# A fused attention and gated-MLP block: a fourth gate/up tile taken out of the attention's filler, GpSimd's sums moved, masks merged, SyncE's DMA issues in written order

## The chip, the cores and the metric

The kernel runs on one core of a Trainium2 chip. Its engines work side by side, each on a queue of its own: TensorE (PE; PEld is its weight load), VectorE (DVE), ScalarE (ACT), GpSimd (POOL), and SyncE (SP), which here issues most of the DMAs. The metric is the device time of one execution in microseconds (us), as a median of several executions; lower is better.

## What is computed

The reference is one transformer block on 2048 tokens of width 640, in float32:

```
xn  = layernorm(x)                                  # no weights
out = x + attention(xn) + mlp(xn)

attention: 32 heads of width 20; a query sees itself and the 255 keys before it
           softmax(q k^T / sqrt(20) under that band mask) v, then @ wo
mlp:       (gelu(xn @ w_gate) * (xn @ w_up)) @ w_down   # inner width 1728, tanh gelu
```

## The kernel before

Every float32 product is made of three products of split operands: a high part and a low part, high x high, low x high and high x low (`dense_steps`, L103). A projection of 640 inputs is five matmuls of 128 rows for each of the three, 15 in all. The 2048 tokens are four chunks of 512. A name such as xh or wqh is a high part, xl or wql the low one.

**Front.** Layer norm and transposes of the four chunks into xh and xl; query/key tiles 0 and 5 are projected for chunks 0 to 2, and the first values.

**Attention** (`attention`, L803) runs 32 units: 8 groups of four heads by 4 chunks. A unit has 14 slots. Its steps are: maxima of the scores (`max_pair`, L473, matmuls L492 on TensorE, reductions L502 on VectorE), the scores again with the maximum taken off and their exponentials in three banks X, Z and Y (`exp_piece`, L543, matmuls L557, ScalarE L559), masks on GpSimd (`clear`, L565, affine_select L572 on the diagonal and L575 on the band's tail), the products with the values (`av_unit`, L578, L600), copies of the sums by ScalarE, their join on GpSimd (L610) and the store (L614, L615). Between these steps the loop pulls matmuls out of a generator, the **filler** (`filler`, L690). It yields the rest of the query/key tiles (five for queries, five for keys, each by four chunks, L107 with ps_d), the values (ps_v), and some of the 14 gate/up tiles of the MLP (`gate_up_fill`, L646). RATE is how many filler matmuls a unit pulls. Before unit 0 there is a **ramp** of twelve slots (L812) with 2 x RAMP = 8 filler matmuls each and up to two maxima pairs in every other slot, and then GAP more filler matmuls.

The order of TensorE, ScalarE, VectorE and GpSimd in this stage is written out by hand (`manual_schedule`, L858): each engine executes in the order in which the code emits. `defer(n, fn)` emits fn n slots later. SyncE's order is left to the framework's scheduler in this stage; in the two later stages it is in written order as well.

A projected query/key tile is saved in three bf16 parts (`save_qk`, L248): ScalarE copies the high part (L277), VectorE takes it off into r (L273), ScalarE copies the middle part (L255), GpSimd makes the lowest one (L259), SyncE stores all three to DRAM (L268). r has one buffer, the target pt has two, and the PSUM tag dn, in which the filler's projections accumulate, has two (`psd`). The loop's loads of query and key parts for unit u+3 (`load_stack`, L458, DMA L467) are emitted in slots 9 and 12 of unit u; those of units 0 to 2 stand ahead of the ramp. Query/key weights are split by ScalarE (L99) and GpSimd (L100) in one piece of 640 columns for tiles 1 and 6, and later ones in five pieces on GpSimd (L641).

GpSimd also makes **sums** of token chunks (`x_sums`, L727, L738): for each of two pairs p of chunks, eighty tensor_tensor operations of 128x256 in all, forty for each pair. Results go to DRAM as td (store L742). The tile tx, in which they are made, has two buffers.

**Pair loop** (`gate_up_pair`, L939, matmuls L957): the gate/up tiles that weren't in the filler, from number NFA to 12. It reads td, and computes two chunks at a time for a gate and an up tile with seven products for eight, so that a call has 54 matmuls of 128x128 by 128x512 where the direct way takes 60. Two calls make a tile. The last gate/up tile (number 13, half wide) is computed at the start of this stage (`gate_up`). Then comes the **down projection** (L1224), in a similar scheme with quarter sums.

Of the kernel before, what the change touches and what calls it, by code (L numbers as in the profile page):

```python
# [13 lines left out]
OP = mybir.AluOpType  # L14
# [16 lines left out]
NS = 14  # L31
RATE = 30.9
LAST = 8
# [3 lines left out]
LAG = 3, 5, 4, 4, 4, 4, 3, 3, 4, 3, 2, 1, 1, 1  # L37
NFA = 3
HD = D // 2
# [3 lines left out]
WARM = 64  # L43
XS0, XSN = 2, 3
HELD = 10, 11, 12
RAMP = 4.0
GAP = 16
VW = 1408
# [19 lines left out]
def block_kernel(ctx, tc, x, wqk, wv, wgu, wdo, wdl, out):  # L68
# [150 lines left out]
    def defer(n, fn, *a):  # L219
        if now[0] is None:  # L220
            fn(*a)
        else:
            at(now[0] + n, fn, *a)
# [24 lines left out]
    def save_qk(t, c, ps):  # L248
# [9 lines left out]
        def lowest():  # L258
            nc.gpsimd.tensor_tensor(out=pt[:, l, :], in0=r, in1=pt[:, 1, :], op=OP.subtract)  # L259
            defer(1, store)  # L260

# [262 lines left out]
    def pieces(c):  # L524
        b = 4 * c
        X = [(b, 0, 0, 384)] + ([(b - 2, 384, 0, 128)] if c else [])
        Y = [(b + 1, 0, 128, 384), (b + 3, 384, 384, 128)]
        Z = ([(b - 1, 0, 0, 256)] if c else []) + [(b + 2, 256, 256, 256)]
        return X, Z, Y

# [34 lines left out]
    def clear(u, bi, js):  # L565
        c = u % NC
        pt = pts[u, bi]
        for p in pieces(c)[bi]:
            for col, diag in diag_tail(*p, c):
                a, n = pt[:, js, col:col + 128], js.stop - js.start  # L570
                if diag:
                    nc.gpsimd.affine_select(out=a, in_=a, pattern=[[0, n], [1, 128]], compare_op=OP.is_ge,  # L572
                                            fill=0.0, base=0, channel_multiplier=-1)
                else:
                    nc.gpsimd.affine_select(out=a, in_=a, pattern=[[0, n], [-1, 128]], compare_op=OP.is_ge,  # L575
                                            fill=0.0, base=-1, channel_multiplier=1)

    def av_unit(u):  # L578
# [38 lines left out]
        defer(3, join)  # L617
        defer(5, store)

# [26 lines left out]
    def gate_up_fill(f, ws, c):  # L646
# [24 lines left out]
        def c5():  # L671
            if now[0] is not None and st.get("tanh", now[0]) >= now[0]:
                defer(1, late, c5)
                return
            nc.vector.scalar_tensor_tensor(st["t"], st["t"], 1.0, st["g"], op0=OP.add, op1=OP.mult)
            defer(1, lambda: nc.sync.dma_start(hd[f][c], st["t"]))

# [12 lines left out]
    def filler():  # L690
# [6 lines left out]
        for s, (kind, i) in enumerate(sets[:-1]):  # L697
            nxt = []
            after = sets[s + 1]
            for c in range(NC):  # L700
                if kind == "qk":
                    if i == 1 and c < 2:
                        for t in range(8 + 4 * c, 12 + 4 * c):
                            yield from proj_v(v0, t)
                    yield from proj_qk(i, ws[0], c)
                    if i == 2 or i == 3 and c == 0:
                        next(prep)
                    yield from proj_qk(i + 5, ws[1], c)
                    if i == 3 and c == 0:
                        next(prep)  # L710
                else:
                    yield from gate_up_fill(i, ws, c)
# [14 lines left out]
    def x_sums(p, k, half):  # L727
# [12 lines left out]
        def store(i):  # L740
            t = live[i]
            defer(2, lambda: nc.sync.dma_start(td[p][i][:, k, half * w:half * w + w], t))  # L742

# [59 lines left out]
    def attention():  # L803
# [4 lines left out]
        for i, (p, k, half) in enumerate((p, k, half) for p in range(NC // 2) for k in range(2) for half in range(2)):  # L808
            for j, fn in enumerate(x_sums(p, k, half)):
                m = 10 * i + j  # L810
                at(NS * (XS0 + m // XSN) + m % XSN, fn)
        for i in range(12):  # L812
# [44 lines left out]

    with tc.manual_schedule(engines=MANUAL | {mybir.EngineType.Pool}):  # L858
        attention()
# [648 lines left out]
```

## Time and profile before

| | us |
|---|---|
| three runs | 1051.27, 1046.38, 1047.88 |
| median | 1047.88 |
| the profiled execution | 1047.3 |
| its span in the profile | 1045.6 |
| mean granted TensorE clock in it | 0.998 |

The stages of the profiled execution, by the matmuls in the chain of work: the front up to some 62.7 us, the ramp to 93.5, the attention's units to 546.3, number 13 to 560.1, the pair loop to 805.1, the down projection to the end at 1045.6.

How to read the rows: a row of the timeline has a start, a duration, the engine, the line of the kernel, the operation with its output and inputs, shapes and a count; in brackets stands how long the engine was idle before it and what released it. "SPq" is SyncE's queue of DMA issues: the row shows the issue, not the transfer. A row of a group has busy time and mean duration in ns behind the first bar, and idle time before these instructions behind the second, with its releasers. A row of waits has the time in all, how often, and the longest. Durations of merged rows overlap a little at their ends, so that a rate is read from the starts of two rows.

### The profile page before, as it was taken

The numbers are of one execution on the slowest core, as the hardware profiler recorded it, in microseconds if no ns is written. First come the engines' busy times: TensorE is split into PE (matmuls) and PEld (weight loads), VectorE is DVE, ScalarE is ACT, GpSimd is POOL, SyncE is SP. The second block draws the span as 40 slices with busy tenths as digits, with TensorE's granted clock in tenths as the row PEclk, the third lists the DMA queues.
The fourth block names the chain that finished last, engine by engine and source line by source line (L and its number), as shares of the span: only waits on it lengthen the run. The fifth ranks groups of instructions, "written<-read, shape, count | busy, mean of one in ns | idle before, by whom it ended". The sixth has DMA issues, their size and how long they took to land.

```text
span 1045.6 us, 25699 instructions
## 1 busy us (share of the span) xinstructions
PE 1033.1 (99%) x9393; PEld 835.1 (80%) x9393; DVE 743.2 (71%) x2018; ACT 527.8 (50%) x1120; POOL 384.5 (37%) x622
## 2 busy tenths in 40 slices
PE   8999999999999999999999999999999999999998
PEld 7887666666787666666678888888888999999998
DVE  7845666677656576777736788775556888888887
ACT  4434666667666666666675232223234554433432
POOL 5122687979766787767470111101110000000000
PEclk9999999999999999999999999999999999999999
DMA  5642355564633364434125575763217874433333
GB/s 193 190 144 93 102 158 170 160 186 141 190 94 100 111 182 139 131 100 148 61 77 194 176 250 205 255 240 113 80 54 252 271 247 136 137 127 121 115 126 105
DMA packets 105192, 158.76 MB, mean 152 GB/s; under 512 B 15420, under 2 KB 60092, under 8 KB 105064
## 3 DMA queue, kind: packets, MB, share of 16 engines
q1 hardware_dynamic: 102680, 150.95, 44.9%
q10 hardware_dynamic: 2384, 6.16, 1.9%
q8 instruction: 74, 1.21, 0.5%
q14 instruction: 54, 0.44, 0.1%
HBM read 101.78 MB, written 54.92 MB: 150 GB/s over the span
## 4 chain that ended last, share of the span: by engine, by line
PE 94%; DVE 4%; ACT 1%; DMA 1%; issue 1%; SPq 0%; POOL 0%; DVEq 0%; ACTq 0%
PE ps_g L957 23%; PE ps L1224 23%; PE ps_d L107 20%; PE ps_e L557 8%; PE ps_v L107 6%; PE ps_o L600 5%; PE ps_m L492 5%; DVE junk L502 2%; PE ps_g L107 1%; DMA wr<-wqk 1%; PE ps_t L185 1%; PE ps_d L356 0%; DVE r L273 0%; DVE xl L194 0%; ACT P L559 0%
## 5 line engine op out<-in xcount | busy, mean ns | idle before, releaser
L502 DVE CUSTOM_DVE_ANT_0 junk<-ps_m,mask 128x320 bf16<-128x320 f32 (+2 forms) x512 | 242.7, 474 | 129.8 <-PE ps_m L492 71.9
L559 ACT ACTIVATE P<-ps_e 128x512 f32<-128x512 f32 (+2 forms) x384 | 198.7, 572 | 69.3 <-PE ps_e L557 68.8
L1224 PE MATMUL ps<-wb,at 128*128 128x320 f32 x999 | 155.9, 309 | 0.0
L1224 PEld LDWEIGHTS ps<-wb,at 128*128 128x128 f32 x999 | 148.9, 188 | 0.2
L572 POOL TENSOR_SCALAR_AFFINE_SELECT P<-P 128x256 f32<-128x256 f32 (+1 forms) x192 | 94.1, 492 | 73.4 <-ACT P L559 70.7
L557 PE MATMUL ps_e<-qs,ks 124*128 124x128 bf16 (+2 forms) x704 | 118.3, 278 | 0.1
L107 PE MATMUL ps_d<-xl,wqh 128*128 128x512 f32 x310 | 98.4, 421 | 0.0
L107 PE MATMUL ps_d<-xh,wqh 128*128 128x512 f32 x310 | 98.2, 421 | 0.0
L107 PE MATMUL ps_d<-xh,wql 128*128 128x512 f32 x310 | 97.6, 418 | 0.0
L100 POOL TENSOR_TENSOR wql<-wr,wqh 128x640 fp32r<-128x640 f32 x12 | 19.2, 1604 | 195.6 <-PE ps_g L957 151.0
L1224 PE MATMUL ps<-wt,at 128*128 128x320 f32 x552 | 88.9, 309 | 0.0
L557 PEld LDWEIGHTS <-ks 124*128 124x128 bf16 x704 | 49.5, 98 | 49.0 <-issue 34.3
L1224 PEld LDWEIGHTS ps<-wt,at 128*128 128x128 f32 x552 | 82.9, 188 | 0.1
L575 POOL TENSOR_SCALAR_AFFINE_SELECT P<-P 128x512 f32<-128x512 f32 (+1 forms) x144 | 76.4, 538 | 16.3 <-ACT P L559 14.6
L1178 ACT ACTIVATE at<-ss 128x512 fp32r<-128x512 f32 x59 | 37.3, 632 | 83.7 <-DVE ss L1062 83.6
L600 PE MATMUL ps_o<-P,v 64*32 64x320 f32 (+4 forms) x2816 | 74.2, 347 | 0.0
L259 POOL TENSOR_TENSOR pt<-r,pt 128x512 bf16<-128x512 f32 x40 | 46.5, 1164 | 67.2 <-ACT pt L255 61.0
L600 PEld LDWEIGHTS ps_o<-P,v 64*32 64x32 f32 x2816 | 50.9, 106 | 21.5 <-issue 0.9
L492 PE MATMUL ps_m<-ks,qs 60*64 60x320 bf16 (+3 forms) x1472 | 64.9, 260 | 3.1 <-DVE mx L502 1.5
L107 PEld LDWEIGHTS ps_d<-xh,wql 128*128 128x128 f32 x310 | 56.0, 189 | 10.1 <-issue 0.9
L492 PEld LDWEIGHTS <-qs 60*64 60x64 bf16 x1472 | 29.2, 105 | 43.6 <-issue 38.0
L107 PEld LDWEIGHTS ps_d<-xh,wqh 128*128 128x128 f32 x310 | 56.0, 189 | 9.7 <-issue 1.6
(195 smaller groups left out, 1968.4 us busy)
## 6 DMA issues: line engine op xcount, KB each, us to landing
hr<-hd SPq DMA_DIRECT2D x104, 128.0 KB
hd<-he SPq DMA_DIRECT2D x50, 256.0 KB
wr<-wgu SPq DMA_DIRECT2D x27, 320.0 KB
qs<-qd SPq DMA_DIRECT2D x64, 120.0 KB
ks<-kd SPq DMA_DIRECT2D x64, 120.0 KB
xi<-x SPq DMA_DIRECT2D x16, 320.0 KB
qs<-qd SPq DMA_DIRECT2D x64, 80.0 KB
ks<-kd SPq DMA_DIRECT2D x64, 80.0 KB
```

The costliest lines, as they stand in the source:

```text
L107: nc.tensor.matmul(ps, a(k), b(k), start=n == 0, stop=n == 3 * nk - 1)
L259: nc.gpsimd.tensor_tensor(out=pt[:, l, :], in0=r, in1=pt[:, 1, :], op=OP.subtract)
L492: nc.tensor.matmul(ps[64 * h:64 * h + 64, col:col + w], q[rows, j, q0:q0 + 64], ks_, start=True, stop=True, tile_position=(64 * r, 64 * h))
L502: nc.vector.tensor_tensor_reduce(out=junk[:, 0:n], in0=ps[:, 320 - n:320], in1=mask[:, 320 - n:320], scale=1.0, scalar=NEG, op0=OP.add, op ...
L557: nc.tensor.matmul(ps[:, col:col + n], k[0:QROWS, j, kc:kc + 128], q[0:QROWS, j, q0:q0 + n], start=True, stop=True)
L559: nc.scalar.activation(pt[:, j, lo:hi], ps[:, lo:hi], AF.Exp, scale=SCALE)
L572: nc.gpsimd.affine_select(out=a, in_=a, pattern=[[0, n], [1, 128]], compare_op=OP.is_ge, fill=0.0, base=0, channel_multiplier=-1)
L575: nc.gpsimd.affine_select(out=a, in_=a, pattern=[[0, n], [-1, 128]], compare_op=OP.is_ge, fill=0.0, base=-1, channel_multiplier=1)
L600: nc.tensor.matmul(os[r][32 * j:32 * j + 32, qa:qb], v[rows, w0_:w0_ + 32], pt[rows, j, col + qa - q0:col + qb - q0], start=r not in begun ...
L957: nc.tensor.matmul(ps, i, j, start=first and n == 0, stop=n == len(work) - 1, skip_group_check=True)
L1178: nc.scalar.activation(hi[:, 3:7], s, AF.Copy)
L1224: nc.tensor.matmul(ps[bank][:, 0:HD], *work[bank][j], start=bank not in begun, stop=final[p, bank] == n and j == len(work[bank]) - 1, skip ...
```

## The change

- NFA goes from 3 to 2: the filler computes gate/up tiles 0 and 1 (beside the query/key tiles and the values), and tile 2 goes to the pair loop, which now starts there. (With number 13, whose weights the filler splits, there were four sets of gate/up weights in it, now three.)
- RATE goes from 30.9 to 26.95 and GAP from 16 to 24.
- In the filler, the values' projections of token tiles 8 to 15 came ahead of query/key tiles 1 and 6 of chunks 0 and 1; now they come behind those of chunks 1 and 2.
- The forty sums of the first pair move from the units into the ramp, three in each slot from slot -13 on; those of the second start in unit 12. Before, all eighty stood three to a unit from unit 2 on.
- `clear` merges the selects of a bank with the same mask into one with a further axis; the two pieces of bank Y change places so that two diagonal blocks lie side by side.
- SyncE's issues in the attention are in written order too, and the stores of query/key parts, of the attention's sums, of the MLP's inner values and of the second pair's token sums are emitted one or two slots later; those of the first pair one slot earlier.

```diff
-RATE = 30.9
+RATE = 26.95
-NFA = 3
+NFA = 2
-XS0, XSN = 2, 3
+XS0, XSN = 12, 3
-GAP = 16
+GAP = 24
...
         def lowest():
             nc.gpsimd.tensor_tensor(out=pt[:, l, :], in0=r, in1=pt[:, 1, :], op=OP.subtract)
-            defer(1, store)
+            defer(3 if now[0] and now[0] > 0 else 1, store)
...
-        Y = [(b + 1, 0, 128, 384), (b + 3, 384, 384, 128)]
+        Y = [(b + 1, 128, 128, 384), (b + 3, 0, 384, 128)]
...
     def clear(u, bi, js):
         c = u % NC
         pt = pts[u, bi]
-        for p in pieces(c)[bi]:
-            for col, diag in diag_tail(*p, c):
-                a, n = pt[:, js, col:col + 128], js.stop - js.start
-                if diag:
-                    nc.gpsimd.affine_select(out=a, in_=a, pattern=[[0, n], [1, 128]], compare_op=OP.is_ge,
-                                            fill=0.0, base=0, channel_multiplier=-1)
-                else:
-                    nc.gpsimd.affine_select(out=a, in_=a, pattern=[[0, n], [-1, 128]], compare_op=OP.is_ge,
-                                            fill=0.0, base=-1, channel_multiplier=1)
+        cuts = sorted(x for p in pieces(c)[bi] for x in diag_tail(*p, c))
+        n = js.stop - js.start
+        for keep in (True, False):
+            cols_ = [col for col, diag in cuts if diag == keep]
+            if not cols_:
+                continue
+            m = len(cols_)
+            assert cols_[-1] == cols_[0] + 128 * (m - 1)
+            a = pt[:, js, cols_[0]:cols_[0] + 128 * m].rearrange("p j (b t) -> p j b t", b=m)
+            sign = 1 if keep else -1
+            nc.gpsimd.affine_select(out=a, in_=a, pattern=[[0, n], [0, m], [sign, 128]], compare_op=OP.is_ge,
+                                    fill=0.0, base=0 if keep else -1, channel_multiplier=-sign)
...
         defer(3, join)
-        defer(5, store)
+        defer(6, store)
...
-            defer(1, lambda: nc.sync.dma_start(hd[f][c], st["t"]))
+            defer(3, lambda: nc.sync.dma_start(hd[f][c], st["t"]))
...
                 if kind == "qk":
-                    if i == 1 and c < 2:
-                        for t in range(8 + 4 * c, 12 + 4 * c):
-                            yield from proj_v(v0, t)
                     yield from proj_qk(i, ws[0], c)
                     if i == 2 or i == 3 and c == 0:
                         next(prep)
                     yield from proj_qk(i + 5, ws[1], c)
                     if i == 3 and c == 0:
                         next(prep)
+                    if i == 1 and c in (1, 2):
+                        for t in range(4 + 4 * c, 8 + 4 * c):
+                            yield from proj_v(v0, t)
...
-            defer(2, lambda: nc.sync.dma_start(td[p][i][:, k, half * w:half * w + w], t))
+            defer(4 if p else 1, lambda: nc.sync.dma_start(td[p][i][:, k, half * w:half * w + w], t))
...
             for j, fn in enumerate(x_sums(p, k, half)):
-                m = 10 * i + j
-                at(NS * (XS0 + m // XSN) + m % XSN, fn)
+                m = 10 * (i % 4) + j
+                at(NS * (XS0 + m // XSN) + m % XSN if p else m // XSN - 13, fn)
...
-    with tc.manual_schedule(engines=MANUAL | {mybir.EngineType.Pool}):
+    with tc.manual_schedule(engines=MANUAL | MANUAL_OUT | {mybir.EngineType.Pool}):
         attention()
```

## The prediction

> **What bounds the kernel now.** First the head of the profile's page and its chain of work that ended last.
>
> ```profile
> span 1045.6 us, 25699 instructions
> ...
> PE 1033.1 (99%) x9393; PEld 835.1 (80%) x9393; DVE 743.2 (71%) x2018; ACT 527.8 (50%) x1120; POOL 384.5 (37%) x622
> ...
> PE 94%; DVE 4%; ACT 1%; DMA 1%; issue 1%; SPq 0%; POOL 0%; DVEq 0%; ACTq 0%
> ```
>
> TensorE is busy 99% of the span and carries 94% of the chain, so only two things move the end: fewer matmuls, or matmuls that wait. The second view is the busy time by stretch; its columns are the stretch, its length, then busy time and count of PE, PEld, DVE, ACT and POOL, granted clock, DMA share, GB/s.
>
> ```profile
> 14.00:17.00 3.00, 2.96 (x15) 2.97 (x16) 2.99 (x9) 2.00 (x6) 3.00 (x4) 0.54 0.07 24
> ...
> 62.70:93.50 30.80, 30.61 (x223) 24.96 (x222) 16.26 (x61) 11.12 (x35) 7.97 (x7) 1.00 0.45 137
> 93.50:119.40 25.90, 25.29 (x278) 17.65 (x276) 16.95 (x68) 17.24 (x45) 11.89 (x23) 1.00 0.35 102
> 119.40:246.40 127.00, 126.46 (x1682) 83.28 (x1679) 87.50 (x321) 88.54 (x181) 108.06 (x177) 1.00 0.55 161
> 246.40:374.70 128.30, 128.01 (x1814) 94.15 (x1820) 80.37 (x319) 85.27 (x221) 91.35 (x164) 1.00 0.44 131
> 374.70:517.40 142.70, 141.23 (x1871) 92.76 (x1875) 103.02 (x371) 92.21 (x188) 97.17 (x166) 1.00 0.41 126
> ```
>
> The ramp is the row 62.70 to 93.50; the units follow. From 62.7 to 517.4 TensorE idles 0.19 + 0.61 + 0.54 + 0.29 + 1.47 = 3.1 us in all. No edit that only shortens waits there can gain more than that. GpSimd is loaded in the units (108.06 of 127.00 us) and nearly idle in the ramp (7.97 of 30.80), but it holds up nobody: POOL has 0% of the chain.
>
> **The fourth gate/up tile.** These rows are from the timeline (start, duration) and from the chain in order of time.
>
> ```profile
> 68.81 1.31 PE L107 MATMUL ps_d<-xh,wql 128*128 128x512 f32 x5
> 69.96 1.30 PE L107 MATMUL ps_d<-xl,wqh 128*128 128x512 f32 x5
> ```
>
> ```profile
> 560.13 244.99 PE ps_g L957 x1080
> ```
>
> Five filler matmuls start 1.15 us after the five before, so one takes 0.230 us. The filler loses 2 matrices x 4 chunks x 15 = 120 of them, 27.6 us. The pair loop gains two calls of 54 products (6+9+6+9+6+9+9), 108 at 244.99/1080 = 0.227, 24.5 us. Net **-3.1 us**. Everything beside these matmuls (ScalarE's and VectorE's GELU, the weight splits) stays under a busy TensorE, as in the ten pairs before it.
>
> **Rate and gap** only place the same filler. A unit loses 3.95 matmuls, 0.9 us, and goes from 142.70/10 = 14.3 to 13.4 us. By the last row VectorE needs 103.02/10 = 10.3 us a unit, ScalarE 9.2, GpSimd 9.7, so nobody else becomes the bound. Idle there is 0.15 us a unit; were it to double in 32 units, +4.7 us. I take 0, and keep +5 as the end.
>
> **Merged masks.**
>
> ```profile
> L572 POOL TENSOR_SCALAR_AFFINE_SELECT P<-P 128x256 f32<-128x256 f32 x128 | 52.8, 413 | 29.4 <-ACT P L559 28.4 <-DMA ks<-kd 0.2
> L575 POOL TENSOR_SCALAR_AFFINE_SELECT P<-P 128x512 f32<-128x512 f32 x80 | 50.4, 644 | 16.3 <-ACT P L559 14.6 <-DMA ks<-kd 1.7
> ```
>
> A select of 256 takes 413 ns, of 512 644 ns: two small ones cost 2 x 413 - 644 = 182 ns more than a double one. Bank X saves one instruction in 24 units, bank Y two in 32: 88 x 0.18 = 16 us of GpSimd, none of it on the path: 0. The swapped columns of Y change no size.
>
> **SyncE in written order, stores later.**
>
> ```profile
> SPq L614 <- POOL ob L610: 65.1, 26, 11.7
> ```
>
> SyncE already stood behind GpSimd's join for 65.1 us without TensorE waiting. What now stands behind a blocked store are the loads of unit u+3, emitted in slots 9 and 12 of unit u and first read in the second half of unit u+1, over half a unit (6.7 us) later. Later stores make the blocks shorter. I take 0; the gain is capped by the 3.1 us above, and the loss shares the +5.
>
> **The sums in the ramp** decide. Forty of the eighty sums, and every projection of query/key tiles 1 and 6 for chunks 0 and 1, now stand in the ramp; the projections of values, which stood between, come after. On the queues (written order of the changed kernel) GpSimd does: the last lowest part of chunk 2, twelve sums, the lowest part of (tile 0, chunk 3), the two splits L100 of tiles 1 and 6, then 28 sums, with a lowest part after each six of them and after the last four. SyncE issues the loads of units 0 to 2 first, and the first td store only behind them.
>
> ```profile
> 62.42 1.17 POOL L259 TENSOR_TENSOR pt<-r,pt 128x512 bf16<-128x512 f32 x1 [2.28 <-ACT pt L255]
> 69.45 1.17 POOL L259 TENSOR_TENSOR pt<-r,pt 128x512 bf16<-128x512 f32 x1 [5.85 <-DMA qs<-qd]
> 70.57 3.10 POOL L100 TENSOR_TENSOR wql<-wr,wqh 128x640 fp32r<-128x640 f32 x2
> ```
>
> ```profile
> 65.55 2.20 SPq L467 DMA_DIRECT2D ks<-kd  x6
> 67.79 2.20 SPq L467 DMA_DIRECT2D qs<-qd  x6
> 70.04 2.62 SPq L467 DMA_DIRECT2D ks<-kd  x6
> ...
> 1037.63 5.45 SPq L1250 DMA_DIRECT2D out<-xr  x4
> ```
>
> ```profile
> 71.09 0.74 PE L107 MATMUL ps_v<-wvh,xh 128*128 128x320 f32 x4
> 71.76 0.36 PE L492 MATMUL ps_m<-ks,qs 60*64 60x64 bf16 x12
> ...
> 82.71 1.29 PE L107 MATMUL ps_d<-xh,wql 128*128 128x512 f32 x5
> ...
> 92.39 0.47 PE L492 MATMUL ps_m<-ks,qs 60*64 60x256 bf16 x16
> ...
> 93.49 0.50 PE L557 MATMUL ps_e<-qs,ks 124*128 124x384 bf16 x2
> ```
>
> ```profile
> L738 POOL TENSOR_TENSOR tx<-tx,xl 128x256 f32<-128x256 f32 x48 | 36.4, 758 | 2.1
> L273 DVE TENSOR_TENSOR r<-ps_d,pt 128x512 f32<-128x512 f32 x40 | 27.5, 687 | 27.5 <-ACT pt L277 25.8 <-POOL pt L259 1.5
> ```
>
> Before, GpSimd had the splits done at 73.7 and TensorE read the first at 82.71. After, tile 1 follows at once: at 71.1 two matmuls (0.46), the reductions' matmuls (0.3), three more (0.69), and at **72.6** TensorE needs the split. GpSimd gets there so: five sums of 0.75 from 63.6 to 67.35; the sixth writes the buffer of the first sum of two (tx has two), whose store SyncE issues only at 72.66 (a load takes it 2.20/6 = 0.37 us), behind the last load. Landing: the last output store was issued by 1043.08 and the span ended at 1045.6, so at most 2.5 us. I take 2.0, bounds 1.4 and 2.5. The sixth and seventh run 75.05 to 76.55, three more to 78.8, the next waits for the third store (issued by 77.0) to 79.0, with its follower to 80.5, the lowest part to 81.6, the split to **83.2**. TensorE waits 10.6 us. The floor, with no store waited for, is 63.6 + 12 x 0.75 + 1.13 + 1.55 = 75.3, a wait of 2.7.
>
> [...]
>
> From there GpSimd sets the pace. r has one buffer: VectorE may read a projection's bank (0.69) only when the lowest part of the projection before is done, and TensorE's next projection but one needs that bank. With 0.75 a sum, 1.13 a lowest part and each store waited for, the lowest parts end at 91.3 (tile 5, chunk 3), 97.1, 104.1 and 110.5. TensorE's starts: tile 1 chunk 1 at 92.1 instead of 89.4, tile 6 chunk 1 at 97.9 (reductions waiting on VectorE about 1.5 us before), the first value projection at 104.9 instead of 102.5, the second at 108.5, the third at 111.3. The ramp ends at 113.8. Undisturbed it would end at 92.39 + 8 x 0.23 = 94.2 (the gap is 8 longer). Loss **+19.6 us**. Floor: from 74.5, 31 sums, 5 lowest parts and the splits are 32.0 us, then 0.7: third value projection at 107.2, loss 15.5. With stores landing in 2.5 us, some eight waits of 0.5 make it about 23.5. Behind the ramp GpSimd has nothing left over but four sums, done before the first selects need it. TensorE's lost time isn't won back, since the units are TensorE's own work.
>
> **Sum.** 1045.6 - 3.1 + 19.6 = 1062.1 us of span. The profiled execution took 1047.3, 1.7 more than its span, and 0.6 less than the median of 1047.88. So 1063.8 beside that execution, and **1064** as a median.
>
> **Rivals.**
>
> (1) GpSimd keeps up: the sums do not stand before the split, or stores land so early that the lowest parts come in time. Then only -3.1 remains: 1044.8. For it: GpSimd's 22.8 idle us in the ramp's row. Against: 40 x 0.75 = 30 us don't fit into them, and the order puts twelve ahead of the split. It decides from the split being done by 72.6. This is the side not slower; within 0.5% (5 us, about what a measurement of this kernel can tell from no change) rather than faster. 10%.
>
> (2) Only the first wait: the single r doesn't bind because the sums catch up while TensorE stands. 1047.9 - 3.1 + 10.6 = 1055.4. Against: by the account above 28 sums and five lowest parts remain after the split, 26.7 us of GpSimd against 94.2 - 72.6 = 21.6 us that are left of TensorE's ramp. 8%.
>
> (3) More than the ramp: units of 13.4 us stall on ScalarE or on SyncE's order (+5), or the clock falls. In the row 14.00 the granted clock is 0.54 after a thin stretch of TensorE; 3 us at 0.54 lose 1.4 us. After a wait of 10.6 us the same may come, but the next wait, 2.7 us, takes it in, so I charge 0. If it came after the last wait too, and with the +5: 1064 + 1.4 + 5 = 1070. 12%.
>
> [...]
>
> (0) The forecast, 1060 to 1068 by its bounds: 70%.
>
> **Range.** 1054 to 1071 takes in (0), most of (2) and (3), and leaves (1) out. Of (1) I give 3 in 10 to more than 0.5% faster. So faster 0.03, within 0.5% 0.08, slower 0.89.
>
> **What would show it.** TensorE's wait for POOL at L100's tile, some 10 us from 72.6, as the largest wait of the trace; SyncE's first td store near 72.7; the first exponential near 115 instead of 93.5; GpSimd busy over 40 of the 50 us from 63.6; units of 13.4 us; 1188 matmuls in the pair loop in 269.5 us. The forecast is wrong if the first wql matmul of tile 1 starts before 76, if lowest parts don't release VectorE's r, or if units grow past 13.7 us.

## The result and the profile after

| | before | after |
|---|---|---|
| median | 1047.13 (1046.26 to 1051.27, four runs) | 1072.82 (1072.32 to 1073.32, four runs) |
| the profiled execution, its span | 1047.3, 1045.6 | 1073.32, 1071.6 |

The ratio is 1.0237 (1.0209 to 1.0266): 25.7 us slower, where the forecast was 1064 in 1054 to 1071. Here and below, medians are of all runs of a kernel, and ratios leave disturbed runs out.

First the head of the page of after: TensorE's share of busy time fell from 99% to 97%. Its 71% of the chain that ended last can't be set beside the 94% of before: followed back from the end, this chain breaks off at 203.03 us, so that its shares add up to some 80% of the span and hold nothing of the ramp.

```profile
span 1071.6 us, 25593 instructions
...
PE 1043.5 (97%) x9381; PEld 840.1 (78%) x9381; DVE 743.7 (69%) x2029; ACT 527.9 (49%) x1120; POOL 375.6 (35%) x526
...
PE 71%; DVE 4%; ACT 3%; issue 1%; DMA 1%; POOL 0%; DVEq 0%; ACTq 0%; SPq 0%
```

The next two fences have the busy time by stretch, first one new row of before (from the first exponential's product to the first matmul of the pair loop), then two of after, the ramp and the same stretch; columns as in the prediction.

```profile
93.49:559.97 466.48, 463.46 (x6092) 319.31 (x6091) 308.69 (x1117) 311.62 (x683) 329.45 (x559) 1.00 0.44 134
```

```profile
62.30:113.30 51.00, 37.55 (x203) 27.66 (x202) 17.30 (x60) 10.69 (x27) 38.34 (x48) 0.83 0.42 132
114.22:560.82 446.60, 439.95 (x5975) 299.30 (x5974) 294.11 (x1103) 304.58 (x674) 287.14 (x419) 1.00 0.44 130
```

From these and the spans, the time divides so (what was forecast counts the GAP's 8 filler matmuls, 1.84 us, to the first line):

| stretch | before | after | difference | forecast |
|---|---|---|---|---|
| start to the first exponential's product | 93.49 | 114.22 | +20.7 | 19.6 + 1.84 = +21.4 |
| from there to the pair loop | 466.48 | 446.60 | -19.9 | -(27.6 + 1.84) = -29.4 |
| pair loop and down projection | 485.63 | 510.78 | +25.1 | +24.5 |
| span | 1045.6 | 1071.6 | +26.0 | +16.5 |

The ramp and the pair loop came as forecast. **The units gave back 9.5 us less than they should**, although TensorE stands idle in that stretch for only 446.60 - 439.95 = 6.7 us (before 3.0). The rest of the loss stands in the rows as busy time, which fell by 23.5 us and not by 29.4.

The ramp, in three views of after's timeline: TensorE, GpSimd, SyncE.

```profile
82.95 2.50 PE L107 MATMUL ps_d<-xh,wql 128*128 128x512 f32 x5 [10.40 <-POOL wql L100]
85.25 2.34 PE L107 MATMUL ps_d<-xl,wqh 128*128 128x512 f32 x5
...
114.22 0.50 PE L557 MATMUL ps_e<-qs,ks 124*128 124x384 bf16 x2
```

```profile
75.01 0.72 POOL L741 TENSOR_TENSOR tx<-xh,tx 128x256 f32<-128x256 f32 x1 [7.88 <-DMA td<-tx]
...
80.25 1.15 POOL L259 TENSOR_TENSOR pt<-r,pt 128x512 bf16<-128x512 f32 x1
81.36 3.04 POOL L100 TENSOR_TENSOR wql<-wr,wqh 128x640 fp32r<-128x640 f32 x2
```

```profile
69.72 2.25 SPq L467 DMA_DIRECT2D ks<-kd  x6
72.07 0.82 SPq L745 DMA_DIRECT2D td<-tx  x2
```

TensorE reads the tile that GpSimd splits at L100 and waits 10.40 us for it (forecast 10.6). GpSimd had stood 7.88 us for a store of its sums, to 75.01 (forecast 75.05), since SyncE came to the first such store at 72.07 only, behind the loads. That 75.01 lies so near 75.05 is in part luck: the store was issued 0.6 us earlier than forecast (72.66), and from the start of its issue to GpSimd's next sum it took 2.94 us where the sum had 0.37 + 2.0. The five matmuls behind the wait start 2.30 us before the next five, twice the usual 1.15: half the clock (granted 0.50 from 82.90 to 87.40; again 0.50 from 102.60 to 104.70, behind the waits around 100 us), and the ramp's mean clock is 0.83. The first exponential's product is at 114.22. Then VectorE's view, the instructions that read a projection's bank:

```profile
81.44 0.69 DVE L273 TENSOR_TENSOR r<-ps_d,pt 128x512 f32<-128x512 f32 x1 [10.75 <-POOL pt L259]
...
90.45 0.69 DVE L273 TENSOR_TENSOR r<-ps_d,pt 128x512 f32<-128x512 f32 x1 [6.52 <-POOL pt L259]
...
109.84 0.69 DVE L273 TENSOR_TENSOR r<-ps_d,pt 128x512 f32<-128x512 f32 x1 [3.03 <-POOL pt L259]
```

These are the first two and the last of five, each released by GpSimd's lowest part: the single r couples TensorE to GpSimd, as forecast (81.6, 91.3, 97.1, 104.1, 110.5). The pair loop's 1188 matmuls take 269.33 us (forecast 269.5):

```profile
560.98 269.33 PE ps_g L960 x1188
```

Now the units. Two views of the chain that ended last, by line, over 204 to 524 us, where both kernels have one, first of before, then of after:

```profile
by line: PE ps_d L107 38.6%; PE ps_e L557 19.0%; PE ps_o L600 12.7%; PE ps_v L107 11.3%; PE ps_m L492 10.5%; DVE junk L502 4.7%; issue 1.3%; PE ps_n L519 0.5%; DVE nm L512 0.3%; DVE nm L511 0.3%; DVE mx L502 0.2%; ACT P L559 0.2%; ACT he L6
```

```profile
by line: PE ps_d L107 29.5%; PE ps_e L557 18.1%; PE ps_o L603 12.1%; PE ps_v L107 11.2%; PE ps_m L492 10.4%; DVE junk L502 5.2%; ACT P L559 4.0%; issue 3.2%; ACT pt L277 1.0%; DMA kd<-pt 0.8%; DVE r L273 0.7%; PE ps_n L519 0.5%; ACT P L610 
```

ScalarE's exponentials had 0.2% of the chain and now have 4.0% (12.8 us), "issue" rose from 1.3 to 3.2%. A share of the chain isn't a loss of the same size, but it says where to look. The same chain of after in order of time shows one such place, and beside it stand TensorE's rows there:

```profile
412.17 0.45 PE ps_m L492 x8
412.62 0.05 issue
412.68 0.59 ACT P L610
413.27 0.49 ACT pt L277
413.76 0.62 ACT wqh L639
414.38 0.98 ACT P L559 x2
415.36 0.04 issue
415.41 0.38 PE ps_e L557 x2
```

```profile
413.65 1.00 PE L107 MATMUL ps_d<-xh,wqh 128*128 128x512 f32 x3
414.92 0.87 PE L557 MATMUL ps_e<-qs,ks 124*128 124x128 bf16 x4 [0.27 <-ACT P L559]
```

Behind the attention-value products and the next reductions (L492) the chain runs along ScalarE's queue: an eviction, a projection's copy (L277), a weight split (L639), two exponentials. Only then can TensorE write a bank of the next exponentials (L557); it has two banks. TensorE's filler lasted to 414.65, and then it stood for 0.27 us: it had slightly too little other work to cover the stretch.

### The profile page after: what moved, and what is told of

Same layout as the page of the kernel before. It is cut to its first block, busy times and chain, and to the rows that moved or that the text cites. A ratio compares the mean times of both kernels' runs of the same rounds, so it can differ in the third digit from the quotient of the medians.

```text
span 1071.6 us, 25593 instructions
## 1 busy us (share of the span) xinstructions
PE 1043.5 (97%) x9381; PEld 840.1 (78%) x9381; DVE 743.7 (69%) x2029; ACT 527.9 (49%) x1120; POOL 375.6 (35%) x526
## 3 DMA queue, kind: packets, MB, share of 16 engines
q8 instruction: 74, 1.21, 0.5%
## 4 chain that ended last, share of the span: by engine, by line
PE 71%; DVE 4%; ACT 3%; issue 1%; DMA 1%; POOL 0%; DVEq 0%; ACTq 0%; SPq 0%
PE ps_g L960 25%; PE ps L1227 19%; PE ps_d L107 10%; PE ps_e L557 6%; PE ps_o L603 4%; PE ps_v L107 3%; PE ps_m L492 3%; ACT P L559 2%; DVE junk L502 2%; PE ps_g L107 1%; DVE ss L1065 1%; DMA hr<-hd 0%; DVE xr L1250 0%; DVE at L1065 0%; DVE wt L1065 0%
## 5 line engine op out<-in xcount | busy, mean ns | idle before, releaser
L578 POOL TENSOR_SCALAR_AFFINE_SELECT P<-P 128x512 f32<-128x512 f32 (+2 forms) x248 | 155.2, 650 | 94.4 <-ACT P L559 93.0
L557 PE MATMUL ps_e<-qs,ks 124*128 124x128 bf16 (+2 forms) x704 | 121.0, 278 | 2.1 <-ACT P L559 0.7
L107 PE MATMUL ps_d<-xh,wql 128*128 128x512 f32 x270 | 89.0, 432 | 10.4 <-POOL wql L100 10.4
L100 POOL TENSOR_TENSOR wql<-wr,wqh 128x640 fp32r<-128x640 f32 x13 | 20.7, 1596 | 217.4 <-PE ps_g L960 192.5
L557 PEld LDWEIGHTS <-ks 124*128 124x128 bf16 x704 | 49.9, 98 | 52.9 <-issue 36.1
L107 PE MATMUL ps_d<-xl,wqh 128*128 128x512 f32 x270 | 88.6, 431 | 0.0
L107 PE MATMUL ps_d<-xh,wqh 128*128 128x512 f32 x270 | 87.3, 425 | 0.4 <-DVE r L273 0.4
L492 PE MATMUL ps_m<-ks,qs 60*64 60x320 bf16 (+3 forms) x1472 | 67.0, 261 | 6.0 <-DVE mx L502 3.6
L989 ACT ACTIVATE hr<-hr 128x512 f32<-128x512 f32 x22 | 13.9, 632 | 111.2 <-DVE hr L963 111.2
L492 PEld LDWEIGHTS <-qs 60*64 60x64 bf16 x1472 | 30.0, 105 | 47.9 <-issue 41.4
L960 PE MATMUL ps_g<-xh,wql 128*128 128x512 f32 x198 | 66.4, 389 | 0.0
L960 PE MATMUL ps_g<-xh,wqh 128*128 128x512 f32 x198 | 66.4, 389 | 0.0
L960 PE MATMUL ps_g<-xl,wqh 128*128 128x512 f32 x198 | 66.3, 389 | 0.0
```

The source lines that it names most:

```text
L100: lo_eng.tensor_tensor(out=lo, in0=raw, in1=hi.bitcast(F32), op=OP.subtract)
L107: nc.tensor.matmul(ps, a(k), b(k), start=n == 0, stop=n == 3 * nk - 1)
L492: nc.tensor.matmul(ps[64 * h:64 * h + 64, col:col + w], q[rows, j, q0:q0 + 64], ks_, start=True, stop=True, tile_position=(64 * r, 64 * h))
L557: nc.tensor.matmul(ps[:, col:col + n], k[0:QROWS, j, kc:kc + 128], q[0:QROWS, j, q0:q0 + n], start=True, stop=True)
L578: nc.gpsimd.affine_select(out=a, in_=a, pattern=[[0, n], [0, m], [sign, 128]], compare_op=OP.is_ge, fill=0.0, base=0 if keep else -1, chan ...
L960: nc.tensor.matmul(ps, i, j, start=first and n == 0, stop=n == len(work) - 1, skip_group_check=True)
```

## The experiments

The theory has two parts: the ramp's loss is GpSimd's forty sums with their stores, the units' loss is the thinner filler, which leaves TensorE waiting for ScalarE's exponentials. The rivals: the ramp's loss needs the denser projections as well; SyncE's written order makes the units' loss; the units are held by VectorE, GpSimd or a third thing. The letters in the expectations are those of their question. In e1 to e4 and e15, A is the sums in the ramp, B the thinner filler, C SyncE's order. From e5 on (but for e15), A is ScalarE's exponentials, B another limit of the units, C the late negations that e5 brought up.

### e1: the sums back in the units

```diff
-XS0, XSN = 12, 3
+XS0, XSN = 2, 3
...
-            defer(4 if p else 1, lambda: nc.sync.dma_start(td[p][i][:, k, half * w:half * w + w], t))
+            defer(4, lambda: nc.sync.dma_start(td[p][i][:, k, half * w:half * w + w], t))
...
-                m = 10 * (i % 4) + j
-                at(NS * (XS0 + m // XSN) + m % XSN if p else m // XSN - 13, fn)
+                m = 10 * i + j
+                at(NS * (XS0 + m // XSN) + m % XSN, fn)
```

> The changed kernel with all eighty sums in the units again, three to a unit from unit 2 on. Theory A (the forty sums in the ramp cost the 19 us that the ramp lost: the weight splits and the lowest parts stand behind them on GpSimd): the ramp ends near 94 instead of 113.3 us, no wait of TensorE for L100's split, time near 1072.8 - 19.4 = 1053.4, up to 1056 if GpSimd's sums slow the thinner units. Rival (the denser query/key projections alone overload GpSimd and r): the ramp still ends after 105 and the time stays above 1064.

Measured 1055.35, ratio 1.0087 (1.0068 to 1.0106). The first exponential's product is back at 96.35; the row of the units' stretch:

```profile
96.35:545.29 448.94, 440.53 (x5975) 299.15 (x5974) 299.84 (x1103) 304.51 (x674) 315.61 (x459) 1.00 0.45 134
```

17.5 us of the change's 25.7 are the sums: the time fell by that much. The units stay long (448.94).

### e2: the fourth tile alone

```diff
-RATE = 30.9
+RATE = 26.95
-NFA = 3
+NFA = 2
-GAP = 16
+GAP = 24
```

> The kernel before with nothing but the fourth tile out of the filler: NFA 2, RATE 26.95, GAP 24. Theory B (the thinner filler leaves ScalarE's and VectorE's delays uncovered in the units, some 0.28 us in each of 31): units of 13.5 us, time near 1047.1 - 3.1 + 8.7 = 1052.7. Rival C (SyncE's written order and the later stores cost the 8.7 us): units of 13.25 us, time near 1044.

This is an edit of the kernel before. Measured 1055.27, ratio 1.0099 (1.0076 to 1.0122).

```profile
93.18:540.83 447.65, 440.15 (x5960) 298.07 (x5958) 302.01 (x1105) 305.31 (x665) 322.13 (x549) 1.00 0.45 135
```

Without loss this stretch would be 466.48 - 27.6 - 1.84 = 437.0, as in the table: the GAP's eight filler matmuls stand in the ramp, which took 32.57 us here (60.61 to 93.18) and 30.78 before (62.71 to 93.49). The stretch is 447.65, so 10.6 us are lost with no sum moved, no mask merged and SyncE as before. And 1055.27 beside e1's 1055.35 says that masks, SyncE's order and the values' place are together worth nothing that shows within these runs (1052.90 to 1059.65 and 1053.27 to 1058.17).

### e3: SyncE's order

```diff
-    with tc.manual_schedule(engines=MANUAL | MANUAL_OUT | {mybir.EngineType.Pool}):
+    with tc.manual_schedule(engines=MANUAL | {mybir.EngineType.Pool}):
```

> The changed kernel with SyncE's order left to the scheduler again in the attention; the order of all other engines is the same, instruction by instruction. Theory B: units stay at 13.5 us, time within 2 us of 1072.8. Rival C: units of 13.25 us, time near 1064.

Measured 1073.44, ratio 1.0257 (1.0242 to 1.0273): within the runs' spread the order costs nothing either way.

### e4: the sums four slots later

```diff
-                at(NS * (XS0 + m // XSN) + m % XSN if p else m // XSN - 13, fn)
+                at(NS * (XS0 + m // XSN) + m % XSN if p else m // XSN - 9, fn)
```

> The changed kernel with the forty sums starting four slots later, behind the two weight splits. Theory A: the first wait of 10.4 us is gone, what remains is GpSimd's pace through r: by GpSimd's queue some 25 sums and four lowest parts stand ahead of the lowest part of tile 1, chunk 1, which ends near 98.6 instead of 109.8; ramp end near 101 to 103, time near 1061. Rival (one late wait is as good as another, since GpSimd's total work sets the ramp's length): time within 3 us of 1072.8.

Measured 1067.32, ratio 1.0197 (1.0181 to 1.0212), between the two. TensorE's waits in its timeline:

```profile
80.02 2.08 PE L107 MATMUL ps_d<-xh,wqh 128*128 128x512 f32 x4 [2.78 <-DVE r L273]
...
116.95 0.64 PE L603 MATMUL ps_o<-P,v 64*32 64x256 f32 x16 [1.08 <-POOL P L578]
118.75 0.73 PE L603 MATMUL ps_o<-P,v 64*32 64x320 f32 x4 [1.17 <-POOL P L578]
```

The wait for the split is gone (the largest in the ramp is 2.78 us) and the first exponential's product is at 103.44, 10.8 us earlier (1.6 of them lie ahead of the ramp). But the sums now last to 113.7, the first selects stand behind them, and unit 0's products with the values wait for P: from their start to those of unit 1 it is 18.05 us (115.09 to 133.14), in after 14.37. A later place did not save the sums: GpSimd's 30 us come due in the ramp or in unit 0.

### e15: the sums alone, in the kernel before

```diff
-XS0, XSN = 2, 3
+XS0, XSN = 12, 3
...
-            defer(2, lambda: nc.sync.dma_start(td[p][i][:, k, half * w:half * w + w], t))
+            defer(2 if p else 1, lambda: nc.sync.dma_start(td[p][i][:, k, half * w:half * w + w], t))
...
-                m = 10 * i + j
-                at(NS * (XS0 + m // XSN) + m % XSN, fn)
+                m = 10 * (i % 4) + j
+                at(NS * (XS0 + m // XSN) + m % XSN if p else m // XSN - 13, fn)
```

> The kernel before with one part of the change alone: the first forty sums on GpSimd in the ramp, four ahead of each step, as in the changed kernel; three gate/up tiles, rate and gap as before, so that the query/key projections of the ramp are less dense. Theory A, that the sums themselves set the ramp: 40 sums of 0.75 us and the lowest parts are about 36 us of GpSimd from 63.6 on against a ramp that ends at 93.5, and the split stands behind a part of them: the first exponential at 104 to 110 instead of 93.5, time 1057 to 1064. Rival, that it takes the denser projections of the fourth tile's gap to make the sums late: at most 3 us, 1051 or less.

Measured 1066.48, ratio 1.0186 (1.0165 to 1.0206), above the expected range of the time, though the first exponential (105.50) lies within its own: the sums last to 110.21 and reach into unit 0, which the expectation had not counted.

```profile
81.98 1.70 PE L107 MATMUL ps_v<-wvh,xh 128*128 128x320 f32 x5 [8.68 <-DVE r L273]
...
105.50 0.50 PE L557 MATMUL ps_e<-qs,ks 124*128 124x384 bf16 x2
...
110.31 0.42 PE L107 MATMUL ps_v<-wvh,xh 128*128 128x320 f32 x1 [3.43 <-DVE r L273]
```

A value projection waits 8.68 us for VectorE's r, which waits for the lowest part behind twelve sums. The rival falls: the sums cost 17.5 us by e1, with the denser projections around them, and 19.5 by e15, without.

### e5: half of each exponential (from e2)

```diff
-            pts[u, bi] = ap.tile([128, 4, C], F32, name="P", tag="P", bufs=3)
+            pts[u, bi] = still[bi]
...
+        hi = (lo + hi) // 2 if u > 3 else hi
         nc.scalar.activation(pt[:, j, lo:hi], ps[:, lo:hi], AF.Exp, scale=SCALE)
```

> The kernel before with the fourth gate/up tile out of the filler (two pairs in it, rate 26.95, gap 24), as in e2_tile_only (median 1055.27), and from unit 4 on each exponential is taken over the left half of its columns alone, so the other half of P holds old values: this leaves out half of the exponentials' elements, and the three P tiles are fixed ones so that the halves that are not written hold something. Theory A, that the thin units lose their time on ScalarE's exponentials and the two PSUM banks that they are read from: the 31 units, 420.1 us from the first attention-value product to the last one in e2_tile_only against 411 if they had shrunk by the filler's matmuls alone, give back most of the 9 us: units at 411 to 414 us, time 1046 to 1050. Rival B, that VectorE's maxima or GpSimd's masks and lowest parts hold the units: units stay at 418 or more, time 1053 or more.

Measured 1053.55, ratio 1.0065 (1.0042 to 1.0089). The units and the largest wait of TensorE:

```profile
93.20:540.00 446.80, 437.08 (x5959) 297.49 (x5958) 310.07 (x1105) 245.61 (x665) 323.10 (x549) 1.00 0.46 135
```

```profile
PE ps_n L519 <- DVE mx L502: 5.8, 5, 1.5
```

Of the 9 us that were to come back, 1 came, and rival B's number was met. But something had come in place of ScalarE: TensorE waits for VectorE at ps_n, the matmul that turns the negated maxima round. e2 has one such wait; VectorE, GpSimd and TensorE there:

```profile
136.82 3.92 DVE L511 TENSOR_SCALAR nm<-mx 128x16 bf16<-128x16 f32 x1
140.77 0.17 DVE L512 SCALAR_TENSOR_TENSOR nm<-mx,nm 128x16 bf16<-128x16 f32 x1
```

```profile
136.44 0.86 POOL L641 TENSOR_TENSOR wql<-wr,wqh 128x128 fp32r<-128x128 f32 x2
137.26 1.27 POOL L610 TENSOR_TENSOR ob<-ob,P 128x512 f32<-128x512 f32 x1
138.50 0.45 POOL L641 TENSOR_TENSOR wql<-wr,wqh 128x128 fp32r<-128x128 f32 x1
138.91 0.62 POOL L572 TENSOR_SCALAR_AFFINE_SELECT P<-P 128x512 f32<-128x512 f32 x1
139.50 1.21 POOL L575 TENSOR_SCALAR_AFFINE_SELECT P<-P 128x512 f32<-128x512 f32 x2
```

```profile
141.41 0.22 PE L519 MATMUL ps_n<-identb,nm 128*128 128x128 bf16 x1 [1.52 <-DVE mx L502]
```

A negation of 16 columns takes 3.92 us instead of 0.17, and ends at 140.74, 0.03 us after the end of seven GpSimd instructions in a row (139.50 + 1.21 = 140.71).

### e6, e7, e8: banks, places of the filler, an eviction on VectorE (from e2)

```diff
-    psx = pp.enter_context(tc.tile_pool(name="psx", bufs=2, space=PSUM))
-    psm = pp.enter_context(tc.tile_pool(name="psm", bufs=4, space=PSUM))
+    psx = pp.enter_context(tc.tile_pool(name="psx", bufs=3, space=PSUM))
+    psm = pp.enter_context(tc.tile_pool(name="psm", bufs=3, space=PSUM))
```

> e2_tile_only (1055.27) with three PSUM banks for exponentials and attention-value products instead of two, and three for the reductions instead of four. Theory A, that an exponential's product waits for one of two banks: it finds a bank 0.5 us earlier, and about 5 of the 9 lost us come back, less what the reductions lose with three banks for two tiles a step (their second step waits for VectorE's 0.3 us read): 1048 to 1054. Rival B, that the reductions and VectorE are what is tight in a thin unit: 1057 or more.

Measured 1147.58, ratio 1.0961 (1.0944 to 1.0979): the reductions need their four banks, and nothing of the exponentials can be read from it.

```profile
PE ps_m L492 <- DVE mx L502: 75.0, 128, 1.5
```

```diff
-                pull_fill(RATE / NS)
+                pull_fill(PLACE[i])
```

> e2_tile_only (1055.27) with the same 26.95 filler matmuls a unit, but not evenly over the 14 slots: 2.9 in slot 0, behind the attention-value products, 2.4 in slots 1 and 2, 1.9 in slots 3 to 10, 1.35 in slots 11 to 13. Theory A: the stretch from the attention-value products to the first exponentials lost most (0.06 to 0.12 us of the 0.3 lost in a unit), since ScalarE has to evict both output banks there before it is done; more filler there covers it, 2 to 4 us come back: 1051 to 1053.5. If every stretch of a unit is as tight as that one, what is taken at the end is lost there: 1054.5 to 1057.

Measured 1056.83, ratio 1.0093 (1.0077 to 1.0109): no gain, as the second case has it.

```diff
-        nc.scalar.activation(oc[:, lo:], os[1][:, lo:], AF.Copy)
+        nc.vector.tensor_copy(oc[:, lo:], os[1][:, lo:])
```

> e2_tile_only (1055.27) with the second of a unit's two output evictions (0.54 us of ScalarE ahead of the first exponentials) on VectorE. Theory A: ScalarE is free 0.5 us earlier and the bank of the second exponential too; 2 to 4 us come back: 1051 to 1053.5. Rival B, VectorE is the tight one: its maxima come 0.5 us later in each unit, 1057 or more.

Measured 1058.00, ratio 1.0108 (1.0089 to 1.0128): theory A fell, and the time is the one that rival B named. TensorE's waits for VectorE's maxima and negations rose from 2.8 + 1.5 us in e2 to 3.6 + 3.0: VectorE has little room in a thin unit either.

### e9, e10: another form of the negation

e9 is made from e2, e10 from e5.

```diff
-                nc.vector.tensor_scalar(nm[:, 0, 0], mx, -1.0, None, op0=OP.mult)
+                nc.vector.scalar_tensor_tensor(nm[:, 0, 0], mx, 0.0, mx, op0=OP.mult, op1=OP.subtract)
```

> e2_tile_only (1055.27, runs from 1052.9 to 1059.65) with the negation of a unit's maxima written as maxima times 0 minus maxima (two tensor inputs) instead of a multiplication by a constant. In e2_tile_only's profile that multiplication of 128x16 took up to 3.92 us instead of 0.175, always ending about 0.03 us after the end of a GpSimd instruction, and TensorE then waited 1.52 us for it once. Theory C, that the one-input form can be kept out by a whole chain of GpSimd instructions, and the two-input form (the next line, never over 1.22 us) by one alone: no negation over 1.3 us, TensorE's wait of 1.5 us gone, units at 418 to 419 us instead of 420.1, time 1052.5 to 1054.5 and the runs nearer to each other. Rival: it isn't the form, the long negations stay, 1055.3 give or take 1.

Measured 1056.55, ratio 1.0074 (1.0049 to 1.0100). Theory C fell as far as the form goes: the two-input negation is as long. Its durations are minimum, median and maximum in ns:

```profile
L511 DVE SCALAR_TENSOR_TENSOR nm<-mx x32: 174/176/3927, 76.7 to 504.8; 128x16 bf16<-128x16 f32 x32
```

> e5_half_exp (1053.55; it leaves out the right half of the exponentials' columns from unit 4 on) with the negation as in e9_other_negation. In e5_half_exp TensorE's waits for exponentials were gone, but five waits for late negations had come, 5.8 us in all. Theory A with C, that ScalarE's exponentials hold the thin units and the late negation only took their place there: both gone, units at 412 to 414.5 us (411 is what the filler's matmuls alone would make of them), time 1046.5 to 1049. Rival B, that a thin unit has a third limit of the same size: units at 417 or more, 1051.5 or more.

Measured 1054.12, ratio 1.0052 (1.0034 to 1.0071): with the long negations, the wait at ps_n stayed too (4.6 us in all), so this could not tell.

### e11, e12: one exponential a slot

```diff
-                if i % 2 and i < 12 and u < NU:
-                    exp_piece(u, i - 1)
-                    if i == 1 and u:
-                        pull_fill(1)
-                        debt[0] -= 1
+                if 0 < i < 12 and u < NU:
+                    if i == 1:
+                        exp_piece(u, 0)
+                        if u:
+                            pull_fill(1)
+                            debt[0] -= 1
                     exp_piece(u, i)
```

Both have e9's negation; e11 is made from e2, e12 from the kernel before.

> e9_other_negation with the exponentials one in each of the slots 2 to 11 instead of two in each odd slot (the first two stay together in slot 1); the filler lies between them, and each finds its PSUM bank about 0.3 us longer free. Theory A: about 5 us of a thin kernel's units are waits of the second exponential of a couple for its bank; 2 to 4 of them come back: 1049.5 to 1052. If the bank isn't what they wait for, the same as e9_other_negation, 1052.5 to 1054.5, or later where the last exponentials and masks come closer to the attention-value products.

> The kernel before (four filler matmuls a unit more) with the negation of e9_other_negation and the exponentials one in a slot as in e11_single_exps. Theory A: its chain of waits has ScalarE's exponentials in 0.5% of the units alone, 2.2 us, and no late negation reached TensorE: 1045.5 to 1047.5. Rival: its units lose time to the couples as well, only less seen: 1043 or less.

Measured 1060.39, ratio 1.0114 (1.0093 to 1.0136), and 1051.91, ratio 1.0034 (1.0019 to 1.0049): both worse than the kernels that they were made from (1056.55 and 1048.47), e12 outside both of its ranges. Spreading the exponentials over the slots brought nothing back, so theory A of e11, the second exponential's wait for its bank, has no support here. Why single ones are worse was not pursued.

### e13, e14, e16: the negation on ScalarE

```diff
             def negate():
-                nc.vector.tensor_scalar(nm[:, 0, 0], mx, -1.0, None, op0=OP.mult)
-                nc.vector.scalar_tensor_tensor(nm[:, 0, 1], mx, -1.0, nm[:, 0, 0], op0=OP.mult, op1=OP.subtract)
+                nc.scalar.activation(nm[:, 0, 0], mx, AF.Copy, scale=-1.0)
...
-            late(negate)
+            defer(1, late, negate)
```

e13 is made from e2, e14 from e5, e16 from the kernel before.

> e2_tile_only (1055.27; 31 units in 420.1 us) with the negation of the maxima on ScalarE, one slot later, and without the second negation, that of the maxima's low part (it leaves out that part: the maxima are subtracted in bf16 alone). In e2_tile_only and e9_other_negation the negation on VectorE took up to 3.9 us, to the end of a chain of GpSimd instructions, in either form, and VectorE's maxima stood behind it. Theory C, that VectorE and GpSimd keep each other out there: ScalarE's negation takes 0.3 us at most each time, TensorE's wait of 1.5 us at unit 2 is gone, units 417.5 to 419, time 1052 to 1054. Rival: TensorE waits there for the maxima themselves; the wait stays, 1055 to 1057.

> e13_neg_on_scalar with the exponentials from unit 4 on over the left half of their columns (it leaves out the other half of the exponentials, and the maxima's low part). In e5_half_exp and e10_half_exp_neg most units were 0.3 to 0.9 us shorter than in e2_tile_only, but a few got 1 to 3 us longer by late negations. Theory A with C: without them units at 411.5 to 414 us, time 1046 to 1049, so that the thin units of the changed kernel lose 5 to 7 us of their 9 to ScalarE's exponentials. Rival B, a third limit: units at 417 or more, 1051.5 or more.

> The kernel before with the negation on ScalarE and without the maxima's low part, as in e13_neg_on_scalar. Theory C: in its thick units the late negations (up to 1.22 us) never reached TensorE, so nothing comes of it: 1046 to 1048. If VectorE's lost time (8.7 us over 64 negations) did reach TensorE by its maxima, up to 1.1 us less: 1045.5 or less.

Measured: e13 1055.68, ratio 1.0085 (1.0061 to 1.0109); e14 1049.18, ratio 1.0015 (0.9997 to 1.0034); e16 1050.38, ratio 1.0026 (1.0014 to 1.0038). The units of e13 and then of e14:

```profile
93.94:541.87 447.93, 440.30 (x5960) 298.21 (x5958) 281.28 (x1043) 308.59 (x696) 323.01 (x549) 1.00 0.45 135
```

```profile
93.94:534.61 440.67, 435.71 (x5959) 296.69 (x5958) 280.54 (x1043) 248.81 (x696) 323.73 (x549) 1.00 0.46 137
```

In e13 the wait of 1.52 us is gone, but the stretch, with 0.22 us more of ScalarE in each unit, is no shorter than e2's: 447.93, and the time missed its range of 1052 to 1054. With half the exponentials on top, 440.67, against 437.0 without any loss: **of the 10.9 us that e13 loses there, 7.3 came back when half of the exponentials' columns from unit 4 on were left out** (6.5 us of the medians, a time 0.2 us above the expected range). So most of what a thin kernel loses hangs on ScalarE's exponentials. What the same edit would do to the kernel before was not measured; TensorE idles there for 3.0 us in all. The chains by line over 125.8 to 524 us, e13 first:

```profile
by line: PE ps_d L107 23.6%; PE ps_e L556 14.5%; PE ps_o L599 10.9%; PE ps_v L107 8.0%; PE ps_m L492 7.9%; ACT P L558 7.2%; DVE junk L502 7.2%; issue 5.4%; SPq L467 1.9%; ACT pt L277 1.3%; DMA od<-ob 1.1%; POOL pt L259 0.9%; POOL P L571 0.7
```

```profile
by line: PE ps_d L107 35.0%; PE ps_e L557 19.5%; PE ps_o L601 14.1%; PE ps_m L492 10.4%; PE ps_v L107 9.0%; DVE junk L502 3.1%; issue 1.5%; DMA qs<-qd 1.1%; DMA ks<-kd 0.8%; PE ps_g L107 0.8%; PE ps_n L518 0.5%; DMA kd<-pt 0.4%; POOL P L573
```

7.2% of ScalarE's exponentials in e13, none among the larger shares in e14, where TensorE's filler is back at 35%. e16 lost 0.26% where nothing was expected, with the same 0.22 us on ScalarE. Its cause was not pursued, but in the same view of its chain ScalarE's exponentials have 1.7%, in that of before 0.1%: even the thick units had little room there.

No kernel here beat the kernel before.

## Why the prediction was wrong

- **What bounds, and the filler against the pair loop:** right. Net -3.1 us; the last stretch measured +25.1 for +24.5.
- **The sums in the ramp:** right in mechanism, places and size: 10.40 us for 10.6 at the split, all five lowest parts within 1.0 us, 20.7 for 21.4 to the first exponential's product. e1 and e15 show that it was the sums, e4 that a better place doesn't save them. The half clock (0.50) behind the wait was taken in by the next waits, as argued; that it would come again later (102.60 to 104.70) was left out of the sum and cost nothing that shows. No run shows the 2.0 us that the sum takes for a store's landing, nor its lower bound of 1.4; what the runs showed in their place is 2.94 us from the start of the first store's issue to the next sum in after, and in the chain a transfer into td of 2.25 us in e15 and one of 1.75 in e13. Two smaller misses: the landing of that first store was longer than taken and its issue earlier, which nearly cancelled, and GpSimd was busy for 37.04 of the 50 us from 63.6, not for over 40.
- **Merged masks, SyncE's order:** right at 0 within the runs' spread (e1 beside e2, e3). The 88 selects fewer saved 11.0 us of GpSimd (159.7 us for 170.7), not 16: a select of 512 columns took 666 ns instead of 644, and one of 1024 columns 1099.
- **"Rate and gap only place the same filler": this step failed.** It took 0.91 us a unit as gained, 0 as lost, because ScalarE's 9.2 us and VectorE's 10.3 fit into 13.4. Busy sums were the wrong test: the filler had covered TensorE's waits for ScalarE's exponentials, and 7.3 of 10.9 us came back when half of these were left out (e14 beside e13). From the first products with the values to those of the last unit, 31 units took 438.69 us before (105.09 to 543.78) and 418.96 after (125.75 to 544.71): a unit went from 14.15 us to 13.51, not to 13.24. The warning sign, units past 13.7 us, did not show: it stood 0.3 us above the 13.4 forecast, which leaves room for 9.6 us in 32 units, about what was lost. How the exponentials hold TensorE is argued from one place in the chain, not shown: ScalarE's work comes in a clump (412.68 to 415.36 above), and TensorE has two banks to work ahead in; but more filler beside the clump (e7), a shorter clump (e8) and exponentials one by one (e11) brought nothing, and e6 could not tell of the banks. The mechanism, units that stall on ScalarE, stood in rival (3), at 12% and +5; the units lost 9.5 in after, 10.6 in e2 alone. With 9.5 the sum would have been 1064 + 9.5 = 1073.5 for the measured 1072.82.
- **Rivals:** (1) and (2) fell to the ramp's waits. (3) was the case by its first part, the units; the clock cost nothing that shows. The range's upper end held +5 and 1.4 and so ended 2 us short.
- **What stays open:** 3.6 of e13's 10.9 us; how much half the exponentials would bring in the thick units of before; and why VectorE's negation lasted through seven GpSimd instructions once in e2 (3.92 us) and through one or two where it was long in before and after (1.23 us at most). How much of after's own loss is ScalarE's was measured in e13's units, with the negation on ScalarE, not in after's (stretches of 447.93 and 446.60).

## What to carry to other kernels

Filler on the bounding engine is also cover: taking 13% of it out of a loop returned 19.9 of 29.4 us here, though no other engine was full on the average of a unit. So busy sums over a unit are not enough to call such a cut free. A place to look is the longest clump of work that stands between two uses of a small ring of buffers, beside what the first engine has to do in the meantime; that this is what counts was not shown here. And idle time of a helper engine is usable only where what stands behind the moved work on its queue (here a weight split, for which TensorE waited 10.40 us, a single buffer's release, the masks) has that much slack.

## What the runs showed of the hardware

VectorE's negations, 128x16 on operands in SBUF, were longer at some places where GpSimd worked. Of the 64 in before (L511 and L512), 45 took 0.174 to 0.176 us and 19 took 0.25 to 1.22; of the 64 in after, 52 took 0.174 to 0.177 and 12 took 0.32 to 1.23. Each of these 31 ended 0.028 to 0.035 us after the end of a GpSimd instruction. In e2 one took 3.92 us and ended at 140.74, 0.03 us after the last of seven GpSimd instructions in a row. That went for both forms: the one-input negation took up to 3.92 us (e2), the two-input one up to 3.93 (e9). On ScalarE the negation of the maxima took 0.215 us at least and 0.258 at most (e13). What makes VectorE's instruction last until then was not shown.
